# Left-factor sums in two rows, and another place for the turns of q and k

## The chip, the cores and the metric

The kernel runs on one core of a Trainium2 chip. A core has TensorE (PE in the profile, its weight loads PEld), VectorE (DVE), ScalarE (ACT), GpSimd (POOL) and SyncE (SP, which here only issues transfers). The engines run side by side, each through its own list of instructions in the order in which the program wrote them, and wait for each other by semaphores. TensorE writes into PSUM banks; in this kernel four are kept for scores, one for turns and values, three for products.

The metric is the device time of one execution in microseconds. The kernel before takes 1606.82 us, the median of three runs (1606.74 to 1608.88).

## The reference, cut to what matters

Attention with normed q and k, then a gated feed-forward layer, all in fp32:

```python
batch, n_heads, seq, head_dim = (8, 12, 448, 64)
n_tokens, d_model, d_ff = (3584, 768, 1536)

# attention, for each of 8 sequences and 12 heads
q_n, k_n = rmsnorm(q, g_q), rmsnorm(k, g_k)
scores = q_n @ k_n.T / sqrt(64)
attn = exp(scores - max(scores)); attn = attn / (sum(attn) + 1e-9)
attn_out = attn @ v                     # heads side by side give x: 3584 x 768

# feed-forward
xn = x / rms(x) * rms_g
g = xn @ w_gate
out = (g * sigmoid(g)) * (xn @ w_val) @ w_out
```

The weights come in as 64-bit floats and have to be turned into 32-bit ones on the chip.

## The kernel before

A block is one sequence; its twelve heads are worked in six pairs, so there are 48 pairs (`NPAIR` is 6). The attention of a block is laid between the steps of the feed-forward layer of the block before it. The first pairs, up to pair 6, have nothing to be laid between: they run alone. Matmuls of the feed-forward layer are done by a Strassen-like scheme in blocks 1 to 7: seven products in place of eight, at the price of sums and differences of the factors on VectorE. Those of the output product's left factors (h) are the `sums` of the change.

Every call of `pe(...)` is one step of TensorE. `after(n, fn)` puts work for other engines behind the n-th step from now. So these two decide the order in each engine's list.

```python
    def after(n, fn):
        due.append((now["t"] + n, fn))

    def pe(fn):
        now["t"] += 1
        fn()
        for item in [d for d in due if d[0] <= now["t"]]:
            due.remove(item)
            item[1]()
```

Turning q or k into the layout that the scores need, a score, and the end of a pair:

```python
    def turn(g, i):
        ...
        ps = (ps_m if todo else ps_f).tile([128, 512], F32, name="tr", tag="m" if todo else "f")
        for t in range(NK):
            nc.tensor.transpose(ps[:, t * 128:(t + 1) * 128], src[:, t * 2 * D:(t + 1) * 2 * D], ident)      # L527
        if i == 0:
            ...
            nc.scalar.activation(st["qT", g], ps[:, 0:S], ACT.Copy, scale=gqk[:, 0:1])                      # L532
            nc.vector.tensor_copy(st["kT", g][:, LAST], ps[:, S:])                                         # L533
        else:
            nc.vector.tensor_copy(st["kT", g][:, FULL], ps[:, FULL])                                       # L535

    def score(g, cs):                 # two heads for each c in cs; one PSUM bank of four for each
        ...
                nc.tensor.matmul(ps[:, 0:S], lhsT=kT[r, c * 128:(c + 1) * 128], rhs=qT[r, :], start=True, stop=True)   # L545
        for (c, j), ps in sc.items():
            ...
            nc.scalar.activation(e, ps[:, 0:S], ACT.Exp, scale=rs[:, n:n + 1])                             # L549
    ...
    def sums(g):                      # the denominators of pair g, then x
        ...                           # matmuls with ones into den (L610)
        if direct(g):
            nc.vector.reciprocal(rd, den[:, 0:S])                                                        # L614
        ...
        nc.vector.tensor_tensor(x, av[:, 0:S], rd, ALU.mult)                                             # L625
```

`rests(g)` (L575 to L590) does the scores of the last 64 rows of pair g and opens the sums `av` (L581) and `den` of pair g-1; `values(g)` (L597) adds the rest of `av`. `squares` takes squares of q and k on ScalarE (L484) and their sums on VectorE (L487); the power and the scaling of q follow on GpSimd (L506, L511). `rms_x` and `norm_x` norm x for the feed-forward layer (L645 to L663).

The conversion of the weights goes in steps too. Each call of `convert()` gives one piece to ScalarE (L740, L741), joins the one before it on VectorE with three instructions, and adds the one before that on GpSimd (L785):

```python
    def join(lo, hi, top):
        nc.vector.tensor_scalar(top.bitcast(F32), top.bitcast(F32), 122879.9921875, 2.0**-15, ALU.min, ALU.max)     # L746
        nc.vector.tensor_scalar(top, top, 3, 0x3FFFFFF8, ALU.logical_shift_left, ALU.bitwise_and)                 # L747
        nc.vector.scalar_tensor_tensor(top, hi, -(2**30), top, ALU.bitwise_and, ALU.bitwise_or)                   # L748

    def turns(n):
        for _ in range(n):
            convert()
```

One group of the feed-forward layer's first part in blocks 1 to 7. The seven products use three PSUM banks in turn, so that p5 takes the bank that p1 and p2 had, once `hand` has read it:

```python
    def quad(b, fp):
        ...
        def hand(gate, value, dst):
            ...
            nc.scalar.activation(th, gate, ACT.Tanh, scale=0.5)                                          # L921
            def rest():
                nc.vector.scalar_tensor_tensor(dst, th, 1.0, gate, ALU.add, ALU.mult)                    # L924
                nc.vector.scalar_tensor_tensor(dst, dst, 0.5, value, ALU.mult, ALU.mult)                 # L925
            after(1, rest)
        ...                           # p1, p6 (adds u2), p2 (hand of bank a), p7 (adds u3, L914), p5, p4, p3
        def sums():
            st["left_sums"] = now["t"]
            for pair in range(len(out_pairs(b))):
                ...
                nc.vector.tensor_tensor(of("S1"), of("A21"), of("A22"), ALU.add)                         # L983
                nc.vector.tensor_tensor(of("S2"), of("S1"), of("A11"), ALU.subtract)                     # L984
                nc.vector.tensor_tensor(of("S3"), of("A11"), of("A21"), ALU.subtract)                    # L985
                nc.vector.tensor_tensor(of("S4"), of("A12"), of("S2"), ALU.subtract)                     # L986

        def p3_last():
            p3()
            after(3, sums)

        return [p1, p6, p2, p7, p5, p4, p3_last]
```

Six groups (`fp`) follow each other in a block. A block has two pairs of rows to sum (`out_pairs`), block 4 one. In block 1 `derive` and `derive_o` (L858, L879) also make differences of the weights on VectorE after most steps, up to three a step; not in the step in which `sums` ran.

The loop over the pairs that run alone:

```python
        if g <= NPAIR:
            if g > 1:
                pe(lambda: turn(g + 1, 0))
                pe(lambda: turn(g + 1, 1))
            pe(lambda: score(g, (0,)))
            squares(g + 2, 0)
            squares(g + 2, 1)
            if g > 1:
                some_rests(g)
            pe(lambda: rests(g))
            pe(lambda: values(g - 1))
            ...
            turns(1 if g == 1 else 3 if g < NPAIR else 0)
            pe(lambda: sums(g - 1))
            pe(lambda: score(g, (1, 2)))
            turns(2 if g == 1 else 0)
            ...
            continue
```

Of the kernel before, what the change touches and what calls it, by code (L numbers as in the profile page):

```python
# [22 lines left out]
NPAIR = H // 2  # L23
# [312 lines left out]
def safe_scores(  # L336
# [42 lines left out]
# [11 lines that stand above are left out]
    NG = B * NPAIR  # L390
# [414 lines left out]
    def out_pairs(b):  # L805
        return (((0, 1),), ((-1, 0), (1, 2)), ((-1, 0), (1, 2)), ((0, 1), (2, 3)))[b % 4]

    def carries(b):
        return b % 4 < 2
# [97 lines left out]
    def quad(b, fp):  # L907

        bank, add = {}, {}
        shift = 64 * (b % 2)  # L910

        def plus(name, ps, other, dst=None):
            add[name] = tmp.tile([128, S], F32, name=name, tag=name, bufs=1) if dst is None else dst
            nc.vector.tensor_tensor(add[name], ps[:, 0:S], add[other], ALU.add)  # L914

        def hand(gate, value, dst):

            th = tmp.tile([128, S], F32, name="th", tag="th", bufs=2)
            n = gate.shape[-1] * (gate.shape[1] if len(gate.shape) == 3 else 1)
            th = th[:, 0:n] if len(gate.shape) == 2 else th.rearrange("p (r n) -> p r n", r=2)  # L920
# [8 lines that stand above are left out]
        def rows(fc):  # L929
            return st["h", b, fc][:, shift:shift + S]  # L930

        def p1():
            bank["a"] = product(b, fp, "A11", "B11")
            add["p1"] = tmp.tile([128, S], F32, name="p1", tag="p1", bufs=1)
            nc.scalar.copy(add["p1"], bank["a"][:, 0:S])

        def p6():
            bank["b"] = product(b, fp, "S2", "T2")
            plus("u2", bank["b"], "p1")

        def p2():
            product(b, fp, "A12", "B21", onto=bank["a"])
            for fc in (fp, fp + NFP):
                st["h", b, fc] = free_h.pop(0)
                if ("h", b - 1, fc) in st:

                    before = st.pop(("h", b - 1, fc))
                    if b % 2:
                        nc.gpsimd.tensor_copy(st["h", b, fc][:, 0:64], before[:, S - 64:S])
                    if carries(b - 1):  # L950
                        at = out_pairs(b - 1)[-1][1] + 1
                        nc.gpsimd.tensor_copy(carried[fc], before[:, at * 128:(at + 1) * 128])
                    free_h.append(before)
            hand(bank["a"][:, 0:HT], bank["a"][:, HT:S], rows(fp)[:, 0:HT])

        def p7():
            bank["c"] = product(b, fp, "S3", "T3")
            plus("u3", bank["c"], "u2")

        def p5():  # L960
            bank["e"] = product(b, fp, "S1", "T1")
            add["cc"] = tmp.tile([128, 2, S], F32, name="cc", tag="cc", bufs=1)
            plus("c22", bank["e"], "u3", dst=add["cc"][:, 1, :])

        def p4():
            bank["d"] = product(b, fp, "A22", "T4")
            plus("c21", bank["d"], "u3")
            after(1, lambda: hand(add["c21"][:, 0:HT], add["c21"][:, HT:S], rows(fp)[:, HT:S]))

        def p3():  # L970
            product(b, fp, "S4", "B22", onto=bank["e"])
            plus("c12", bank["e"], "u2", dst=add["cc"][:, 0, :])
            after(1, lambda: hand(add["cc"][:, :, 0:HT], add["cc"][:, :, HT:S], rows(fp + NFP).rearrange("p (r n) -> p r n", r=2)))

        def sums():

            st["left_sums"] = now["t"]
            for pair in range(len(out_pairs(b))):
                if fp == 0:
                    st["so", b, pair] = {name: room_so[3 * pair + i].rearrange("p (c n) -> p c n", c=NFP)  # L980
                                         for i, name in enumerate(("S1", "S2", "S4"))}
                of = lambda name: left_o(b, pair, name, fp)
# [4 lines that stand above are left out]

        def p3_last():
            p3()
            after(3, sums)  # L990

        return [p1, p6, p2, p7, p5, p4, p3_last]

# [248 lines left out]
    def some_rests(g):  # L1242
        b, hp = divmod(g, NPAIR)
        if g == 1:
            norm_rests(0, 4, NPAIR)
        elif hp in (3, 4):
            norm_rests(b + 1, 3 * (hp - 3), 3 * (hp - 2))
# [5 lines that stand above are left out]
# [22 lines left out]
    for g in range(NG + 1):  # L1275
        b, hp = divmod(g, NPAIR)
        if g:
            load_pair(g + 3)
        if hp == 2:
            for i in range(2):  # L1280
                load_rests(b + 1, i, nc.sync)
            load_v_rests(b + 1)
        if g == 0:
            pe(lambda: score(0, (0,)))
            pe(lambda: rests(0))
            pe(lambda: score(0, (1,)))
            pe(lambda: turn(1, 0))
            pe(lambda: score(0, (2,)))
            norm_rests(0, 2, 4)
            squares(2, 0)  # L1290
            squares(2, 1)
            pe(lambda: turn(1, 1))
            for _ in range(3):
                convert()
            load_pair(3)
            load_v(2)
            convert()
            load_rows()
            continue
        if g <= NPAIR:  # L1300
            if g > 1:
                pe(lambda: turn(g + 1, 0))
                pe(lambda: turn(g + 1, 1))
            pe(lambda: score(g, (0,)))
            squares(g + 2, 0)
            squares(g + 2, 1)
            if g > 1:
                some_rests(g)
            pe(lambda: rests(g))
            pe(lambda: values(g - 1))  # L1310
            if g == 1:
# [3 lines that stand above are left out]
            load_v(g + 2)  # L1315

            turns(1 if g == 1 else 3 if g < NPAIR else 0)
            pe(lambda: sums(g - 1))
            pe(lambda: score(g, (1, 2)))
            turns(2 if g == 1 else 0)  # L1320
            if g == 2:
                bound()
            continue

        if g == NPAIR + 1:
            pe(lambda: score(g, (0,)))
            pe(lambda: rests(g))
            pe(lambda: rms_x(0))
        else:
            pe(lambda: (rests(g), score(g, (0,)) if g < NG else None))  # L1330
        pe(lambda: values(g - 1))
        load_v(g + 2)
        if g == NPAIR + 1:
            pe(lambda: score(g, (1,)))
            pe(lambda: norm_x(0))
            pe(lambda: score(g, (2,)))
        pe(lambda: sums(g - 1))
        if g == NPAIR + 1:
            begin(0, 15)
            turns(3)  # L1340
        elif g < NG:
            pe(lambda: score(g, (1, 2)))
        st["block"] = now["t"]
        if hp:
            fill()
# [4 lines that stand above are left out]
            fill()  # L1350
            pe(lambda: turn(g + 1, 1))
            fill()
            continue
        fill(3)
        pe(lambda: turn(g + 1, 0))
        fill(1)
        pe(lambda: rms_x(b - 1))
# [3 lines that stand above are left out]
        fill(len(todo))  # L1361
        begin(b - 1, 16)
        pe(lambda: norm_x(b - 1))
        fill()
# [41 lines left out]
```

## Time and profile before

| what | before |
|---|---|
| time | 1606.82 us |
| span of the profiled run | 1605.0 us |
| granted clock of TensorE, mean | 0.997 |
| TensorE, matmuls | 1572.9 us, 98% |
| VectorE | 873.0 us, 54% |
| GpSimd | 659.5 us, 41% |
| ScalarE | 471.0 us, 29% |
| pairs that run alone | about 17 to 84 us |
| feed-forward of block 0, first product | first matmul (L1121) at 97.13 us |
| feed-forward of blocks 1 to 7, first product (L902) | 303.3 to 1543.5 us |

In the rows of a timeline the first number is the start in us from the start of the span, the second the duration; x12 means twelve records, of which an fp32 matmul leaves two. A bracket at the end gives the idle time of that engine just before, and what ended it. In the list of waits each row names who waited, for whom, and then us in total, how often, and the longest. In a row of windows the columns are the window, its length, the busy time of TensorE, its weight loads, VectorE, ScalarE and GpSimd (number of instructions in brackets), the granted clock, and the share and rate of the transfers.

### The profile page before, as it was taken

The numbers are of one execution on the slowest core, as the hardware profiler recorded it, in microseconds if no ns is written. First come the engines' busy times: TensorE is split into PE (matmuls) and PEld (weight loads), VectorE is DVE, ScalarE is ACT, GpSimd is POOL, SyncE is SP. The second block draws the span as 40 slices with busy tenths as digits, with TensorE's granted clock in tenths as the row PEclk, the third lists the DMA queues.
The fourth block names the chain that finished last, engine by engine and source line by source line (L and its number), as shares of the span: only waits on it lengthen the run. The fifth ranks groups of instructions, "written<-read, shape, count | busy, mean of one in ns | idle before, by whom it ended". The sixth has DMA issues, their size and how long they took to land.

```text
span 1605.0 us, 21557 instructions
## 1 busy us (share of the span) xinstructions
PE 1572.9 (98%) x7286; PEld 1113.5 (69%) x7286; DVE 873.0 (54%) x1556; ACT 471.0 (29%) x940; POOL 659.5 (41%) x712
## 2 busy tenths in 40 slices
PE   8989999999999999999999999999999999999998
PEld 4334445777756887568875688668885688859974
DVE  6878889578833566335563254535563345513531
ACT  6745555232222222222222222323322222101010
POOL 6857886645423443244433443344542342000000
PEclk9999999999999999999999999999999999999999
DMA  7647565866756554465544655484554544457652
GB/s 211 203 138 223 191 210 164 258 214 208 255 177 186 154 150 145 133 193 154 150 135 133 203 156 158 142 259 135 158 153 123 169 141 136 126 162 222 174 151 57
DMA packets 261996, 273.28 MB, mean 170 GB/s; under 512 B 78836, under 2 KB 258804, under 8 KB 261876
## 3 DMA queue, kind: packets, MB, share of 16 engines
q1 hardware_dynamic: 260948, 271.61, 56.3%
q8 instruction: 60, 0.98, 0.3%
q14 instruction: 60, 0.49, 0.1%
q10 hardware_dynamic: 800, 0.20, 0.1%
q0 software_dynamic: 128, 0.00, 0.0%
HBM read 232.40 MB, written 39.32 MB: 169 GB/s over the span
## 4 chain that ended last, share of the span: by engine, by line
PE 80%; DVE 5%; POOL 0%; DMA 0%; issue 0%; SPq 0%; ACT 0%; DVEq 0%; POOLq 0%
PE ff L902 40%; PE ff L1093 22%; PE sc L545 6%; PE av L597 5%; PE sc L575 2%; PE den L610 2%; PE tr L527 1%; PE ff L1003 1%; DVE top L747 1%; DVE top L748 1%; DVE top L746 0%; PE ff L1121 0%; DVE rd L618 0%; DVE h L925 0%; DVE h L924 0%
## 5 line engine op out<-in xcount | busy, mean ns | idle before, releaser
L902 PE MATMUL ff<-x,w 128*128 128x224 f32 x1878 | 381.5, 354 | 3.7 <-DVE h L925 2.6
L902 PEld LDWEIGHTS ff<-x,w 128*128 128x128 f32 x1878 | 351.3, 190 | 19.2 <-issue 11.7
L555 POOL TENSOR_TENSOR es<-e 128x448 f32<-128x448 f32 x82 | 92.1, 1144 | 493.7 <-ACT e L549 493.7
L902 PE MATMUL ff<-xs,w 128*128 128x224 f32 x1374 | 281.4, 353 | 2.9 <-DVE w L858 2.9
L902 PEld LDWEIGHTS ff<-xs,w 128*128 128x128 f32 x1374 | 258.1, 190 | 6.3 <-issue 6.0
L562 POOL TENSOR_TENSOR es<-es,e 64x448 f32<-64x448 f32 (+1 forms) x164 | 191.8, 1180 | 6.3
L618 DVE RECIPROCAL rd<-rd 128x448 f32<-128x448 f32 x41 | 121.0, 2952 | 112.2 <-ACT rd L617 112.2
L549 ACT ACTIVATE e<-sc,rs 128x448 f32<-128x448 f32 x288 | 161.9, 634 | 47.6 <-PE sc L545 46.2
L1093 PE MATMUL ff<-w,h 128*128 128x384 f32 x498 | 167.8, 487 | 0.6 <-ACT p L1072 0.6
L1093 PE MATMUL ff<-w,raw 128*128 128x384 f32 x468 | 159.5, 487 | 0.3 <-DVE y L1065 0.3
L1093 PEld LDWEIGHTS ff<-w,h 128*128 128x128 f32 x498 | 93.5, 190 | 64.5 <-issue 1.3
L545 PE MATMUL sc<-qT,kT 64*128 64x448 f32 x576 | 136.1, 572 | 1.9 <-ACT e L549 0.7
L1093 PEld LDWEIGHTS ff<-w,raw 128*128 128x128 f32 x468 | 87.6, 190 | 60.9 <-issue 2.6
L597 PE MATMUL av<-e,vt 128*64 128x448 f32 x576 | 118.8, 548 | 0.0
L506 POOL TENSOR_TENSOR rs<-ms,mhalf 128x12 f32<-128x12 f32 (+1 forms) x50 | 114.2, 2284 | 4.2
L1121 PE MATMUL ff<-x,w 128*128 128x448 f32 x288 | 113.6, 548 | 0.0
L545 PEld LDWEIGHTS sc<-qT,kT 64*128 64x128 f32 x576 | 52.8, 185 | 78.9 <-issue 70.0
L914 DVE TENSOR_TENSOR cc<-ff,u 128x448 f32<-128x448 f32 x84 | 52.4, 623 | 91.6 <-PE ff L902 91.4
L1121 PEld LDWEIGHTS ff<-x,w 128*128 128x128 f32 x288 | 54.1, 193 | 51.9 <-issue 50.1
L597 PEld LDWEIGHTS av<-e,vt 128*64 128x64 f32 x576 | 37.1, 136 | 75.6 <-issue 73.6
L785 POOL TENSOR_TENSOR w<-top,raw 128x384 int32<-128x384 int32 x63 | 67.0, 1078 | 39.2 <-DVE top L748 25.9
L631 POOL TENSOR_TENSOR ss<-ss,rd 128x448 f32<-128x448 f32 x40 | 46.2, 1155 | 80.1 <-ACT rd L630 79.3
(132 smaller groups left out, 1814.4 us busy)
## 6 DMA issues: line engine op xcount, KB each, us to landing
w<-kept SPq DMA_DIRECT2D x511, 192.0 KB, 2.7
w<-kept_o SPq DMA_DIRECT2D x296, 192.0 KB, 2.7
kept<-w SPq DMA_DIRECT2D x89, 192.0 KB, 3.9
qk<-in_q_dram SPq DMA_DIRECT2D x48, 192.0 KB, 2.9
qk<-in_k_dram SPq DMA_DIRECT2D x96, 96.0 KB, 3.2
vt<-in_v_dram SPq DMA_DIRECT2D x48, 192.0 KB, 2.5
raw<-in_moe_w_gate_dram SPq DMA_DIRECT2D x24, 384.0 KB, 4.7
raw<-in_moe_w_val_dram SPq DMA_DIRECT2D x24, 384.0 KB, 4.5
```

What stands on the lines that cost most here:

```text
L506: nc.gpsimd.tensor_tensor(st["rs", g][:, cols], ms, mhalf[:, cols], ALU.pow)
L545: nc.tensor.matmul(ps[:, 0:S], lhsT=kT[r, c * 128:(c + 1) * 128], rhs=qT[r, :], start=True, stop=True)
L549: nc.scalar.activation(e, ps[:, 0:S], ACT.Exp, scale=rs[:, n:n + 1])
L555: nc.gpsimd.tensor_tensor(es, st["e", g, 0, j], st["e", g, 1, j], ALU.add)
L562: nc.gpsimd.tensor_tensor(es[r], es[r], e[r], ALU.add)
L597: nc.tensor.matmul(av[own(j), 0:S], lhsT=vt[:, j, c], rhs=st["e", g, c, j], start=False, stop=(c == NK - 1), skip_group_check=True)
L618: nc.vector.reciprocal(rd, rd)
L785: nc.gpsimd.tensor_tensor(data(key).bitcast(I32), top, lo, ALU.add)
L902: nc.tensor.matmul(bank[:, w * HT:(w + 1) * HT], lhsT=wt[:, c * 128:(c + 1) * 128], rhs=x[:, c, :], start=onto is None and w == c == 0, st ...
L914: nc.vector.tensor_tensor(add[name], ps[:, 0:S], add[other], ALU.add)
L1093: nc.tensor.matmul(ps, lhsT=left_o(b, which, LEFT_O[name], c), rhs=data(("wo", b, name, c)), start=first and c == 0, stop=c == NFP - 1, sk ...
L1121: nc.tensor.matmul(bank[w][:, 0:S], lhsT=data(key)[:, c * 128:(c + 1) * 128], rhs=st["x", 0, half][:, c, :], start=half == c == 0, stop=ha ...
```

## The change

Two things are changed. The sums of the output product's left factors, up to eight instructions in one place, are given to VectorE in two rows of four: the first row at the third step after a group's last product, the second two steps later. It is meant to let what other engines wait for come between them. And the pairs that run alone go back to another order: the turns of q and k, which stood between the scores c=1,2 of one pair and c=0 of the next, come after the latter. With it, three conversions of weights stand behind the scores of pair 6 and no longer behind the start of block 0, and in pair 7 the residual scores come before score c=0.

```diff
-        def sums():
+        def sums(pair):
             st["left_sums"] = now["t"]
-            for pair in range(len(out_pairs(b))):
+            if pair < len(out_pairs(b)):
@@ def p3_last():
             p3()
-            after(3, sums)
+            after(3, lambda: sums(0))
+            after(5, lambda: sums(1))
@@ for g in range(NG + 1):
         if g <= NPAIR:
-            if g > 1:
-                pe(lambda: turn(g + 1, 0))
-                pe(lambda: turn(g + 1, 1))
             pe(lambda: score(g, (0,)))
             squares(g + 2, 0)
             squares(g + 2, 1)
             if g > 1:
+                pe(lambda: turn(g + 1, 0))
                 some_rests(g)
+                pe(lambda: turn(g + 1, 1))
             pe(lambda: rests(g))
@@
             pe(lambda: score(g, (1, 2)))
-            turns(2 if g == 1 else 0)
+            turns(2 if g == 1 else 3 if g == NPAIR else 0)
@@
+        pe(lambda: (rests(g), score(g, (0,)) if g < NG else None))
         if g == NPAIR + 1:
-            pe(lambda: score(g, (0,)))
-            pe(lambda: rests(g))
             pe(lambda: rms_x(0))
-        else:
-            pe(lambda: (rests(g), score(g, (0,)) if g < NG else None))
@@
         if g == NPAIR + 1:
             begin(0, 15)
-            turns(3)
```

## The prediction

> **What bounds the kernel now.** I read four views of the profile of before: the shares of busy time, the waits of TensorE, the timeline around the longest of these waits, and the timeline around one of the short ones. The busy shares and the chain come first:
>
> ```profile
> PE 1572.9 (98%) x7286; PEld 1113.5 (69%) x7286; DVE 873.0 (54%) x1556; ACT 471.0 (29%) x940; POOL 659.5 (41%) x712
> ...
> PE 80%; DVE 5%; POOL 0%; DMA 0%; issue 0%; SPq 0%; ACT 0%; DVEq 0%; POOLq 0%
> ```
>
> TensorE is busy in 1572.9 of 1605.0 us, and its matmuls fill 80% of the chain. The change leaves out no matmul, so all that it can give or take is in the 32 us in which TensorE stands still, and in what a stop costs afterwards. The view of waits names them (us in total, times, longest):
>
> ```profile
> PE tr L527 <- DVE kT L533: 7.7, 2, 6.9
> PE ff L902 <- DVE w L858: 2.9, 2, 1.5
> PE ff L902 <- DVE h L925: 2.6, 3, 1.0
> ...
> PE ff L902 <- DVE u L914: 1.1, 1, 1.1
> ```
>
> What is left out are waits of 1.9 us and less, most of them in the first 84 us. The reader is to see one wait of 6.9 us, three of up to 1.0 us on h (L925), and two that the change hardly touches (w, L858). Now the long wait, in the timeline (start, duration, instruction):
>
> ```profile
> 112.32 0.91 DVE L746 TENSOR_SCALAR xs<-xs 128x384 f32<-128x384 f32 x1
> 113.26 1.17 DVE L747 TENSOR_SCALAR xs<-xs 128x384 int32<-128x384 int32 x1
> 114.46 1.36 DVE L748 SCALAR_TENSOR_TENSOR xs<-raw,xs 128x384 int32<-128x384 int32 x1
> 115.75 0.21 DVE L533 COPY kT<-tr 128x64 f32<-128x64 f32 x1
> ...
> 116.01 0.90 PE L527 MATMUL tr<-ident,qk 128*128 128x128 f32 x3 [6.90 <-DVE kT L533]
> 116.71 8.74 PE L1121 MATMUL ff<-x,w 128*128 128x448 f32 x18
> ```
>
> The copy L533 frees the one PSUM bank in which q and k are turned. It takes 0.21 us, but stands behind six joins of converted weights (L746 to L748, one join is one of each) that VectorE began only at 100.96: 14.8 us of backlog. The windows show what follows the stop:
>
> ```profile
> 109.00:116.00 7.00, 0.11 (x1) 0.00 (x0) 6.86 (x9) 0.99 (x2) 5.98 (x6) 0.82 0.77 221
> 116.00:121.00 5.00, 4.99 (x10) 2.74 (x11) 4.86 (x11) 0.03 (x1) 4.68 (x5) 0.57 0.24 87
> ```
>
> Columns after the length: TensorE, its weight loads, VectorE (6.86 of 7), ScalarE, GpSimd, then the granted clock: 0.57 for the five us after the stop. The same three turns and 18 matmuls, 9.37 us here (116.01 to 125.38), took about 7.2 us at 224.6 to 231.8 at full clock. So the stop costs 6.9 + 2.1 = 9.0 us. Last, one of the short waits on h:
>
> ```profile
> 563.14 0.28 DVE L983 TENSOR_TENSOR raw<-h,h 128x128 f32<-128x128 f32 x1
> 563.46 0.29 DVE L984 TENSOR_TENSOR raw<-raw,h 128x128 f32<-128x128 f32 x1
> 563.66 0.28 DVE L985 TENSOR_TENSOR h<-h 128x128 f32<-128x128 f32 x1
> 563.87 0.28 DVE L986 TENSOR_TENSOR raw<-h,raw 128x128 f32<-128x128 f32 x1
> ...
> 564.62 0.39 DVE L925 SCALAR_TENSOR_TENSOR h<-h,ff 128x224 f32<-128x224 f32 x1
> ...
> 565.05 2.54 PE L902 MATMUL ff<-x,w 128*128 128x224 f32 x12 [0.85 <-DVE h L925]
> ```
>
> The four sums of the second row pair, 563.14 to 564.07, stand directly before h, which frees the PSUM bank that p5 waits for.
>
> **What the Trainium skill says.** "TensorE: Matmul & The Clock Gate", section "What's actually happening", says that an idle window of about 3.4 us puts the array back to half clock, and that a busy window of that length brings it back. The trace agrees: after 6.9 us of rest the clock is 0.57, and it is 1.00 from 121. The waits of up to 1.9 us are too short for it. "SBUF — State Buffer", section "SBUF: two separate sides", says that VectorE and GpSimd share a port pair which one of them holds for a whole instruction. The trace fits: L747 takes 0.36 us alone and 1.06 us while GpSimd adds (1.01 us). That is why six joins of 0.35 + 0.36 + 0.56 take 14 us here and not 8. The same TensorE page, section "Architectural detail: the array is 16× 32×32, not 1× 128×128", calls VectorE strictly first in, first out. So the place of an instruction in the list is what counts, and the change moves places.
>
> **The change part by part.** No instruction is added or removed on any engine. Three things move.
>
> *A, the order in pairs that run alone (17 to 84 us).* Before: scores c=1,2 of pair g; both turns of pair g+2; score c=0 of g+1. After: all six scores in a row, then the turns. From the starts of the scores (25.96, 36.17, 49.36, 60.95, 72.61, 83.27) the periods of before are 10.2, 13.2, 11.6, 11.7 and 10.7 us. The last has no wait, so 10.66 us is TensorE's own work, and the three middle ones hold 2.5, 0.9 and 1.0 us of waits. On ScalarE the exponentials of score c=0 now come before the copy of q and the square of x, which waits for VectorE's x. So the squares for the next norm no longer stand behind that wait, and VectorE's gap of 1.57 us ahead of L487 closes. In exchange kT (L533) waits for q's copy, which comes 0.8 us later. Worked through with the durations of before:
> - pair 2: the turn's wait of 1.9 us on the scaled q (L511, GpSimd) falls under the score, but av waits for x, and x comes after three joins and the reciprocal (2.95 us), which begin 0.3 us later: +0.3;
> - pairs 3 and 4: the joins start 0.7 us sooner, x is there when av asks for it, and a wait of about 0.1 us for a score's bank is new: -0.8 and -0.9;
> - pair 5: no wait to win, the same 0.1 us: +0.1.
>
> Sum -1.3 us.
>
> *B, three conversions move from after the start of block 0 (97 us) to pair 6 (about 87 us).* There VectorE stands idle for 2.92 and 3.73 us (ahead of L647 and L663). Three joins of 1.27 us fit between x at 87.1 and the norm at about 91.5; GpSimd's adds and power then end near 93, and TensorE asks for them only at 93.9. What it costs: the residual scores now stand ahead of score c=0 of pair 7, so av waits for x at 87.1 about 1.4 us instead of having other work; before lost 0.6 us at this place, and a row of small shifts leaves the first matmul of block 0 some 0.6 us later. What it gives: of six joins three are gone from the backlog. VectorE is free at about 101.7, does three joins (4 us alone, 6 with GpSimd in the way) and one h (0.6), and reaches L533 between 106.5 and 108.5. TensorE asks at 109.1 + 0.6 = 109.7. I leave 0.5 us of wait. The stop of 9.0 us goes, clock and all: +0.6 - 9.0 + 0.5 = -7.9 us.
>
> *C, the sums in two rows.* Blocks 1 to 7 have six groups each. Block 4 has one row pair, so 36 groups change. In each, four sums of 0.28 us (0.93 us in a row) go from before h of the gate to behind p5's own addition. h frees p5's bank 0.93 us sooner: the waits of 0.85, 0.72 and 1.04 us become about 0, 0 and 0.1: -2.5. The wait of 1.1 us on u in block 1 (406.91) has the same eight sums ahead of it: -1.0. The derived weights in block 1 lose one step, and their waits (2.9 us) I leave as they are. In the other 32 groups no one waits, and nothing is gained. Sum -3.5 us, of which I count 3.
>
> Together -1.3 - 7.9 - 3 = -12.2 us, which gives 1594.6; I write 1595.
>
> **The rivals.** *First: the stop at 116 returns elsewhere.* VectorE is busy 46.05 of 50 us between 100 and 150, and a TensorE that is 8 us ahead may catch up with it again, or ScalarE's copy of q may be late. For it: the whole stage is full. Against it: the joins that went earlier are work taken out of this stage, and kT L535 at 120.4 is needed only at 125.4. It would leave -5 instead of -12: 1602. *Second: the pairs alone get slower.* The order in before was perhaps chosen to give the exponentials (0.55 us each) time before the score's banks are used again. If each of five pairs waited 0.6 us for a bank, A would be +3, the total -8: 1599. Against it: the first exponential ends 1.6 us after the row of scores begins, when TensorE is just through with the four. *Third: the pair 7 seam.* If norm, power and scaling of x come late, block 0 starts up to 3 us later, and the total is -9: 1598. *Fourth: the second row of sums lands before an addition that TensorE then waits for.* For the addition after p4 there are 2.27 us of matmul between, against 1.15 us of sums; worth at most +1.
>
> **Range and chances.** All rivals at once would eat the gain and give about 1605; with the waits in A wholly gone (4.5 us) and nothing left of B and C it would be some 1588. So 1587 to 1605 for 8 in 10. For 2% either way 32 us are needed, as much as all of TensorE's standstill: 1% each.
>
> **What would show it.** A: scores of pairs 3 to 6 begin 10.7 us apart. B: no wait on kT L533 above 3 us, and a clock near 1.00 in the windows between 109 and 121; the first matmul of block 0 at 95 to 98 us. C: the waits on h and u vanish from TensorE's list. What would make it wrong: a new wait above 3 us in block 0, which brings the half clock with it, or a first matmul of block 0 after 99 us.

## The result, and the profile after

The changed kernel takes 1596.8 us (median of 4 runs, 1596.38 to 1597.13), against 1607.05 us before (4 runs, 1606.74 to 1608.88). The ratio is 0.9934, with a 95% interval of 0.9917 to 0.9951: 10 us faster, within 2%. I had said 1595, in a range of 1587 to 1605.

The profile of the changed kernel, first the shares of busy time, then the list of TensorE's waits (us in total, times, longest):

```profile
PE 1571.9 (99%) x7286; PEld 1113.4 (70%) x7286; DVE 872.6 (55%) x1556; ACT 470.3 (29%) x940; POOL 660.1 (41%) x712
```

```profile
PE ff L902 <- DVE cc L914: 1.5, 3, 0.5
...
PE av L581 <- issue: 1.2, 1, 1.2
PE rb L657 <- POOL rs L649: 1.0, 1, 1.0
PE tr L527 <- DVE kT L533: 0.9, 1, 0.9
```

The same 7286 matmuls take the same time within 1.0 us. The wait of 6.9 us on kT is gone (the one of 0.9 is another, late in block 0), and so are the waits on h and u. Three rows of these are new: av without a named releaser and rb on rs, both in pair 7, and three waits on cc, the additions for c22. A fourth new row, left out here, is one of 1.7 us of av in pair 2, where the turn had waited 1.9 us before. The place of the former stop, in the timeline of the changed kernel (behind the sums its line numbers are one higher than before, so L1122 is L1121 of before):

```profile
107.79 1.38 DVE L748 SCALAR_TENSOR_TENSOR xs<-raw,xs 128x384 int32<-128x384 int32 x1
109.10 0.21 DVE L533 COPY kT<-tr 128x64 f32<-128x64 f32 x1
...
109.87 0.49 PE L527 MATMUL tr<-ident,qk 128*128 128x128 f32 x3
110.20 6.93 PE L1122 MATMUL ff<-x,w 128*128 128x448 f32 x18
```

VectorE is done with kT 0.6 us before TensorE asks for the bank. The 18 matmuls take 6.93 us; before they took 8.74. The windows of the same stretch (length, TensorE, weight loads, VectorE, ScalarE, GpSimd, clock, transfers) have the clock at 1.00 and TensorE full:

```profile
109.00:116.00 7.00, 7.00 (x22) 3.67 (x21) 6.79 (x16) 1.45 (x3) 6.68 (x7) 1.00 0.21 73
116.00:121.00 5.00, 5.00 (x28) 1.64 (x28) 4.90 (x7) 3.00 (x7) 5.00 (x5) 1.00 0.57 172
```

To see where the time went I compared the start of the same TensorE instruction in both traces. There are 48 turns of the last rows (L531), one for each pair, and further marks where a stage begins:

| mark | before, us | after, us | after less before |
|---|---|---|---|
| scores c=1,2 of pair 1 | 25.96 | 26.39 | +0.43 |
| scores c=1,2 of pair 6 | 83.27 | 82.33 | -0.94 |
| first matmul of block 0 | 97.13 | 98.05 | +0.92 |
| residual scores of pair 8, after the former stop | 125.38 | 117.06 | -8.32 |
| turn in block 1, ahead of its last change | 394.25 | 386.00 | -8.25 |
| next turn | 425.62 | 417.00 | -8.62 |
| turn in block 2, after its wait on h | 593.17 | 584.41 | -8.76 |
| turn in block 3, after its wait on h | 790.99 | 782.09 | -8.90 |
| last turn, block 6 | 1323.15 | 1314.26 | -8.89 |
| last matmul, block 7 | 1597.20 | 1587.36 | -9.84 |
| end of the span | 1605.0 | 1595.3 | -9.7 |

So the pairs alone (A) gave 1.37 us, the seam at pair 7 took 1.86, the stop gave 9.24 (0.07 came back after it), and the sums (C) gave 1.6 up to the last matmul, of which 0.95 behind the last turn. The first 0.43 us are not from the change; they are taken up at the end. Without them the changed kernel is 10.3 us ahead at the last matmul.

### The profile page after: what moved, and what is told of

It reads as the page before. It is cut to its first block, busy times and chain, and to the rows that moved or that the text cites. A ratio compares the mean times of both kernels' runs of the same rounds, so it can differ in the third digit from the quotient of the medians.

```text
span 1595.3 us, 21559 instructions
## 1 busy us (share of the span) xinstructions
PE 1571.9 (99%) x7286; PEld 1113.4 (70%) x7286; DVE 872.6 (55%) x1556; ACT 470.3 (29%) x940; POOL 660.1 (41%) x712
## 4 chain that ended last, share of the span: by engine, by line
PE 78%; DVE 7%; DMA 1%; issue 1%; POOL 0%; SPq 0%; ACT 0%; DVEq 0%; POOLq 0%
PE ff L902 39%; PE ff L1094 22%; PE sc L545 6%; PE av L597 5%; PE sc L575 2%; PE den L610 2%; PE tr L527 1%; DVE top L747 1%; DVE top L748 1%; DVE top L746 1%; PE ff L1004 1%; DVE rd L618 1%; DVE h L925 0%; DVE h L924 0%; DMA w<-kept_o 0%
## 5 line engine op out<-in xcount | busy, mean ns | idle before, releaser
L1122 PE MATMUL ff<-x,w 128*128 128x448 f32 x288 | 111.8, 541 | 0.0
L1122 PEld LDWEIGHTS ff<-x,w 128*128 128x128 f32 x288 | 53.3, 190 | 50.8 <-issue 49.0
L631 POOL TENSOR_TENSOR ss<-ss,rd 128x448 f32<-128x448 f32 x40 | 46.6, 1165 | 82.7 <-ACT rd L630 82.7
L935 ACT COPY p<-ff 128x448 f32<-128x448 f32 x42 | 22.4, 533 | 192.6 <-PE ff L902 192.6
```

Of the source, the lines that this page charges most:

```text
L631: after(1 if soon else 4, lambda: (nc.gpsimd.tensor_tensor(ss, ss, rd, ALU.add), st.update({("summed", b): hp})))
L1122: nc.tensor.matmul(bank[w][:, 0:S], lhsT=data(key)[:, c * 128:(c + 1) * 128], rhs=st["x", 0, half][:, c, :], start=half == c == 0, stop=ha ...
```

## The experiments

Each kernel ran in several rounds beside the kernel before on the same chip. The ratios are to that kernel, with a 95% interval. None leaves out a part of the computation; one adds matmuls that nobody reads. After the first 12 us of the program the executions stand up to 3 us apart, so a step of 1 to 2 us is read from the marks inside the traces, counted from the first scores on, and not from medians alone.

My theory after the result: the stop on kT went because three joins went, and the clock with it; the seam costs more than I had said; the sums bring less because a new wait took the place of the old. The rivals were that the turns and exponentials of the pairs removed the stop, and that the sums had brought all of the listed 3.5 us, with the loss elsewhere.

**The sums alone.**

```diff
 # the kernel before
-            after(3, sums)
+            after(3, lambda: sums(0))
+            after(5, lambda: sums(1))
```

> The kernel before with the sums in two rows of four and nothing else of the change. Theory (the shifts of TensorE's marks between the two traces): the waits on h and u go, but waits of about 0.5 us on the addition for c22 (cc, L914) come in their place, so it gains 1.4 us and takes 1605.6. Rival (the list of waits alone): every wait on h and u that went is gained, 3.5 us, 1603.5; then the rest of the loss against my prediction lies in the seam at pair 7. The wait of 6.9 us on kT L533 stays in both.

Measured: 0.9992 (0.9984 to 1.0001), 1607.2 us against 1608.69. By the marks, blocks 1, 2, 3 and 6 gain 0.23, 0.16, 0.15 and about 1.0 us, 1.5 in all. The interval of the times includes no gain at all, so the marks alone show it. The waits on cc are in its list too (1.6 us, three times). The theory holds and the rival falls: nothing is hidden in the seam, since this kernel has the seam of before. The timeline of the changed kernel shows what takes the gain back in block 2:

```profile
555.08 0.39 DVE L925 SCALAR_TENSOR_TENSOR h<-h,ff 128x224 f32<-128x224 f32 x1
...
555.52 2.54 PE L902 MATMUL ff<-x,w 128*128 128x224 f32 x12
556.31 0.61 DVE L914 TENSOR_TENSOR u<-ff,u 128x448 f32<-128x448 f32 x1
556.84 0.28 DVE L983 TENSOR_TENSOR raw<-h,h 128x128 f32<-128x128 f32 x1
...
557.56 0.28 DVE L986 TENSOR_TENSOR raw<-h,raw 128x128 f32<-128x128 f32 x1
557.77 0.54 DVE L450 TENSOR_REDUCE msr<-sq 128x6 f32<-128x384 f32 x1
...
558.23 0.61 DVE L914 TENSOR_TENSOR cc<-ff,u 128x448 f32<-128x448 f32 x1
...
558.90 2.54 PE L902 MATMUL ff<-xs,w 128*128 128x224 f32 x12 [0.51 <-DVE cc L914]
```

The product at 555.52 no longer waits for h. But a turn of q lies between p2 and p7 in this group, so that the fifth step is p7 and not p5. The second row of sums (556.84 to 557.77) therefore stands, with a reduce of squares (L450), ahead of the addition for c22 (cc). p3 accumulates onto the bank that this addition has to read first, and waits 0.51 us. A correction belongs here: I wrote that p5 takes the bank of p1 and p2. By the order of the additions in both traces the product that waited for h is p4.

**All but the sums.**

```diff
 # the changed kernel
-            after(3, lambda: sums(0))
-            after(5, lambda: sums(1))
+            after(3, sums)
```

> The changed kernel with the sums back in one row of eight. Theory: everything up to the first matmuls after the former stop is as in the changed kernel, 8.3 us sooner than before, and the waits on h and u return: 1598.2. Rival: the two parts lean on each other (the sums' gain is there only when block 0 hands on an earlier VectorE), then it would take 1597 or below, or above 1600.

Measured: 1598.39 us, 0.9938 (0.9925 to 0.9952). The waits on h (2.6 us, three times) and u (1.1) are back. By the marks it is 8.7 us ahead of before at the last matmul. With the 1.5 us of the run before that makes 10.2 of the 10.3; the two parts do not lean on each other.

**The conversions alone.**

```diff
 # the kernel before
-            turns(2 if g == 1 else 0)
+            turns(2 if g == 1 else 3 if g == NPAIR else 0)
@@
             begin(0, 15)
-            turns(3)
```

> The kernel before with the three conversions given behind the scores of pair 6 in place of behind the start of block 0; the turns, the order in pair 7 and the sums stay as before. Theory: this alone takes the stop of 9 us away (wait on kT L533 below 1 us, clock 1.00 between 109 and 121), and costs about 1 to 1.9 us at the seam, because VectorE's joins now stand ahead of the norm of x and GpSimd's adds ahead of its power: 1599. Rival: the stop goes because the turns and exponentials of the pairs were moved, then it stays here and the time is 1607 or more.

Measured: 1599.89 us, 0.9952 (0.9938 to 0.9965), 8.8 us less than before by the medians. By the marks, which leave out the start, 7.4 of the 10.3 us come from moving three conversions. Its list of TensorE's waits:

```profile
PE ff L902 <- DVE h L925: 2.6, 3, 1.0
...
PE rb L657 <- POOL rs L649: 1.4, 1, 1.4
...
PE tr L527 <- DVE kT L533: 0.8, 1, 0.8
```

The stop is gone though turns and exponentials stand as before, so the rival falls. The wait of rb on rs is there: the seam's price comes with the conversions. By the marks (+0.38 ahead of the seam, +2.25 behind it) it is 1.87 us, the same as in the changed kernel.

**The turns alone.**

```diff
 # the kernel before, pairs 2 to 6
-            if g > 1:
-                pe(lambda: turn(g + 1, 0))
-                pe(lambda: turn(g + 1, 1))
             pe(lambda: score(g, (0,)))
@@
             if g > 1:
+                pe(lambda: turn(g + 1, 0))
                 some_rests(g)
+                pe(lambda: turn(g + 1, 1))
```

> The kernel before with only the turns of q and k after score c=0 in pairs 2 to 6; conversions, pair 7 and sums stay as before. Theory: 1.4 us between the scores of pair 1 and pair 6 are gained, the stop of 6.9 us and its slow clock stay: 1605.5. Rival: the order of before was there to give the exponentials time, and without it the pairs get slower: 1608 to 1610.

Measured: 1606.48 us, 0.9987 (0.9981 to 0.9994), 2.2 us less than before. From pair 1's scores (28.12) to pair 6's (84.04) it is 55.92 us, in place of 57.31: 1.39 us. Only pair 1 got slower, by 0.24 us; the others did not miss the time that the old order gave the exponentials. Another 0.6 us comes between there and pair 8, where this kernel has nothing changed. The stop is 6.90 us in this trace as in before, but the 18 matmuls behind it take less time here than in before (8.74), and in the trace of the sums alone, with the same stop, more:

```profile
117.47 8.18 PE L1121 MATMUL ff<-x,w 128*128 128x448 f32 x18
```

```profile
118.99 9.24 PE L1122 MATMUL ff<-x,w 128*128 128x448 f32 x18
```

Windows of 1 us show where the slow clock lies, first with the turns alone, then with the sums alone:

```profile
113.00:114.00 1.00, 0.00 (x0) 0.00 (x0) 0.99 (x2) 0.00 (x0) 1.00 (x2) 0.58 0.64 152
119.00:120.00 1.00, 1.00 (x3) 0.59 (x2) 0.93 (x3) 0.00 (x0) 0.92 (x2) 0.51 0.00 0
```

```profile
116.00:117.00 1.00, 0.00 (x0) 0.00 (x0) 0.97 (x2) 0.00 (x0) 1.00 (x2) 0.91 0.83 275
123.00:124.00 1.00, 1.00 (x3) 0.41 (x3) 0.97 (x3) 0.29 (x1) 0.92 (x3) 0.68 0.00 0
```

All windows between the two of a trace have 0.50, so a window of 0.58 has the half clock for 0.84 of its 1.00 us. The half clock begins 3.3 us after TensorE stopped here, 4.4 in before and 5.4 with the sums alone, and lasts 6.8 us in all three. The later it begins, the more of it falls on the matmuls behind the stop: 3.2, 4.3 and 5.4 us. Half of that is 1.6, 2.2 and 2.7 us, and by so much the turn and the matmuls are longer than in the changed kernel. So one and the same stop has three prices. The 0.6 us here are no gain of the change, and the trace of the sums alone loses 0.5 us in the same way.

**TensorE kept at work during the stop.**

```diff
 # the kernel before
             fill()
+            if g == NPAIR + 1:
+                keep_warm(28)          # 28 matmuls ident x ident, 128 columns, into a bank of the scores; nobody reads it
             pe(lambda: turn(g + 1, 1))
```

> The kernel before with 28 matmuls of 128 columns, whose result nobody reads, put on TensorE ahead of the turn that waits 6.9 us (some 6.7 us of work at 0.24 us each), so that TensorE does not stand still while VectorE works off its joins. Nothing is taken out. Theory: the stop costs its own length and 2.1 us of half clock afterwards; with the clock held at 1.00 the turns and 18 matmuls take 7.2 us in place of 9.4 and the kernel gains about 2 us. Rival: those matmuls were slow because VectorE or the weights' transfers held them, then their 9.4 us and the time stay, or the time grows by what the added matmuls overrun.

Measured: 1605.09 us against 1607.81, 0.9984 (0.9977 to 0.9991), with 28 matmuls more. Timeline and windows of this kernel:

```profile
111.04 6.41 PE L1245 MATMUL warm<-ident 128*128 128x128 f32 x56
118.15 0.55 PE L527 MATMUL tr<-ident,qk 128*128 128x128 f32 x3 [0.69 <-DVE kT L533]
118.53 6.93 PE L1121 MATMUL ff<-x,w 128*128 128x448 f32 x18
```

```profile
109.00:116.00 7.00, 7.00 (x51) 5.91 (x50) 6.86 (x8) 2.03 (x4) 6.05 (x6) 1.00 0.76 225
116.00:121.00 5.00, 4.30 (x24) 2.98 (x23) 4.90 (x9) 0.01 (x1) 4.68 (x6) 1.00 0.55 164
```

VectorE's backlog is as it was (6.86 of 7 us), and TensorE still gets its bank only when kT is copied, but the 18 matmuls that follow take 6.93 us and not 8.74. The marks move from +2.09 ahead of the stop to +0.02 behind it: 2.07 us, against the 2.1 that I had put down for the slow clock. That part of the stop's 9 us is shown to be the clock. The size, 2.1 us, is that of the one trace of before.

**One, two and three conversions.**

```diff
 # the kernel before, with n = 1 or 2 (3 is the run above)
-            turns(2 if g == 1 else 0)
+            turns(2 if g == 1 else n if g == NPAIR else 0)
@@
             begin(0, 15)
-            turns(3)
+            turns(3 - n)
```

> The kernel before with one of the three conversions moved ahead to pair 6. Theory: each joined piece is worth about 2.2 us of backlog where GpSimd is in the way, so the wait on kT falls to about 4.7 us, still long enough for the slow clock: gain 2.3 us. Rival: the stop is set by something other than the number of joins (the copy of q on ScalarE, a transfer), then it stays near 6.9 us.

> The kernel before with two of the three conversions moved ahead to pair 6. Theory: the wait on kT falls to about 2.5 us, which is too short for the slow clock, so the step from one to two conversions is worth more than the step from none to one: 2.2 + 2.1 us, a gain of 6.5 us in all. Rival: a loss of clock in proportion to the wait, then each step is worth the same 3 us.

Measured: one gives 1605.61 us, 0.9986 (0.9980 to 0.9993); two give 1602.78 us, 0.9971 (0.9961 to 0.9982). The turn after the stop, in the timeline with one conversion moved and then with two:

```profile
114.88 0.90 PE L527 MATMUL tr<-ident,qk 128*128 128x128 f32 x3 [4.96 <-DVE kT L533]
115.57 8.22 PE L1121 MATMUL ff<-x,w 128*128 128x448 f32 x18
```

```profile
112.67 0.55 PE L527 MATMUL tr<-ident,qk 128*128 128x128 f32 x3 [3.02 <-DVE kT L533]
113.06 8.62 PE L1121 MATMUL ff<-x,w 128*128 128x448 f32 x18
```

The wait falls from 6.90 to 4.96, 3.02 and nothing, so the number of joins sets it. From the end of x (L625) to the copy L533 VectorE takes 14.7, 12.8, 10.8 and 7.2 us with none to three moved: 1.9 us for each of the first two, 3.7 for the third. The marks behind the stop move by -2.1, -3.9 and -7.4 us (with the seam, which costs 0.35 us with one or two and 1.87 with three). The step I expected from one to two comes only from two to three. A loss of clock in proportion to the wait (the rival) is not what happens either: the slow clock takes 1.65 us of the turn and the 18 matmuls with one conversion moved, 1.75 with two and none with three. A wait of 3.02 us was still enough for the slow clock, as the windows of the kernel with two moved show:

```profile
110.00:112.00 2.00, 0.00 (x0) 0.00 (x0) 1.97 (x2) 0.00 (x0) 2.00 (x2) 1.00 0.80 230
112.00:114.00 2.00, 1.33 (x6) 0.80 (x7) 2.00 (x6) 0.00 (x0) 1.85 (x3) 0.91 0.74 254
114.00:116.00 2.00, 2.00 (x4) 0.97 (x3) 1.93 (x5) 0.00 (x0) 1.83 (x3) 0.50 0.04 14
116.00:118.00 2.00, 2.00 (x5) 0.95 (x4) 1.90 (x6) 0.80 (x2) 1.92 (x2) 0.74 0.00 0
```

TensorE is back at 112.67, and the clock drops after that, to 0.50.

**The second row of sums later.**

```diff
 # the changed kernel
-            after(5, lambda: sums(1))
+            after(7, lambda: sums(1))
```

> The changed kernel with the second row of sums at the seventh step in place of the fifth, so that it stands behind the addition for c22 (cc) in the crowded groups too. Theory: the waits of 0.5 us on cc L914 go, three of them, and the kernel gains 1 to 1.5 us on the changed one: a ratio to before of about 0.9927. Rival: the row meets another addition there (c21, c12) and TensorE waits for that instead: no gain, or a loss of up to 1 us.

Measured: 1596.43 us, 0.9929 (0.9915 to 0.9942). On another chip than the changed kernel's first runs this does not tell them apart, so both ran again, side by side:

> The changed kernel once more, beside the next three and the kernel before on one chip, so that steps of 1 to 2 us can be read: a ratio to before of 0.9934, as measured first, if the first microseconds of the program (which start up to 2 us apart in the traces) average out.

> The changed kernel with the second row of sums at the seventh step, once more. Theory: TensorE's marks in the two traces say that it gains 2.1 us on the changed kernel in blocks 1 to 3. Rival: the medians of the two on different chips differed by 0.4 us only; if the gain was the first microseconds' scatter, the two are equal here.

Measured: the changed kernel 1598.39 us, 0.9929 (0.9915 to 0.9942); with the later row 1594.99 us, 0.9916 (0.9902 to 0.9929). The intervals overlap, the marks are clear: against the trace of the changed kernel they agree within 0.04 us up to block 1, and then stand at -0.5, -1.3 and -2.07 after the crowded groups of blocks 1, 2 and 3. The timeline of the kernel with the later row, block 2 again:

```profile
555.80 0.61 DVE L914 TENSOR_TENSOR u<-ff,u 128x448 f32<-128x448 f32 x1
...
556.79 0.61 DVE L914 TENSOR_TENSOR cc<-ff,u 128x448 f32<-128x448 f32 x1
...
557.71 2.44 PE L902 MATMUL ff<-xs,w 128*128 128x224 f32 x12
558.13 0.28 DVE L983 TENSOR_TENSOR raw<-h,h 128x128 f32<-128x128 f32 x1
```

cc comes before the row, p3 starts at once, and no wait on cc is left in the list. So the waits on h and u were worth what I had said (0.92 us in block 2: 0.14 in the changed kernel, 0.78 more here); from block 1 to the last matmul this kernel gains 3.6 us on before, where the list of waits had given 3.5. The fifth step was the wrong place to collect it.

**The seam.**

```diff
 # the kernel with the later row
-            turns(2 if g == 1 else 3 if g == NPAIR else 0)
+            turns(2 if g == 1 or g == NPAIR else 0)
@@ pair 7
             pe(lambda: rms_x(0))
+            turns(1)
```

> As the one before, and of the three conversions behind pair 6 the third is given after the norm of x in pair 7. Theory: of the 1.9 us that the seam lost, 1.0 is TensorE's wait for GpSimd's power (rb on rs L649), which stands behind joins and adds; one join fewer ahead of it brings about 1 us. Rival: the third join then delays the scaling of x or the copy L533 by as much, and nothing is gained.

```diff
 # and with it, pair 7
-        pe(lambda: (rests(g), score(g, (0,)) if g < NG else None))
         if g == NPAIR + 1:
+            pe(lambda: score(g, (0,)))
+            pe(lambda: rests(g))
             pe(lambda: rms_x(0))
             turns(1)
+        else:
+            pe(lambda: (rests(g), score(g, (0,)) if g < NG else None))
```

> As the one before, and pair 7 has the order of before again: score c=0 ahead of the residual scores, so that TensorE has work while av waits for x. Theory: the other 0.9 to 1.2 us of the seam's loss goes too, 2 us below the changed kernel with the later row, 4 us below the changed kernel. Rival: TensorE only comes sooner to the next wait (rb on rs, or the turn on L533), and it is no faster than the one before.

Measured: 1593.73 us, 0.9907 (0.9892 to 0.9922), and 1593.34 us, 0.9901 (0.9886 to 0.9916). In before TensorE meets no wait at the norm of x for block 0, in the changed kernel it does (timelines, before first):

```profile
89.99 0.16 DVE L647 TENSOR_SCALAR ms<-msx 112x4 f32<-112x4 f32 x1 [2.92 <-PE msx L645]
...
93.24 0.60 PE L657 MATMUL rb<-ident,rs 112*128 112x112 f32 x4
```

```profile
92.39 0.56 DVE L748 SCALAR_TENSOR_TENSOR top<-raw,top 128x384 int32<-128x384 int32 x1
92.86 0.15 DVE L647 TENSOR_SCALAR ms<-msx 112x4 f32<-112x4 f32 x1
...
94.17 0.60 PE L657 MATMUL rb<-ident,rs 112*128 112x112 f32 x4 [1.03 <-POOL rs L649]
```

The third join holds ms until 92.86, and rb waits for the power behind it. With that join after ms, rb starts at 92.89 without a wait, and the marks gain 1.1 us: the theory. The old order in pair 7 takes away the wait of av too (1.2 us), but gains only about 0.4 us more by the marks (from +0.03 ahead of the seam to -1.47, against -0.17 to -1.27), and its median is 0.4 us lower, within the intervals. Most of it goes, as the rival says, into the next step: a wait of 0.5 us on the sum of squares (msx on ss L631) is new. The last version is the fastest of the study.

## Why the prediction was right

- *What bounds it.* Right: the matmuls took the same time in both kernels, and all of the difference is in TensorE's waits and in its clock.
- *A, -1.3 us.* Right in sum, -1.37, but by some luck, for its parts were not. Pair 1 lost 0.24 us, which I had not counted (a score waits for its bank); pairs 2 to 5 gave 0.05, 1.14, 0.22 and 0.20 where I had +0.3, -0.8, -0.9 and +0.1. Pair 4 still waits for x, and its residual scores can't run beside av. So the scores of pairs 3 to 6 begin 10.45, 11.44 and 10.46 us apart, and my sign of 10.7 came in two of three.
- *B, the stop, -8.5 us.* Right, and slightly too small: -9.24 from the first matmul to the residual scores of pair 8. Both terms are shown apart: 6.9 us of joins and 2.07 us of clock, the latter the size in one execution. The 0.5 us of wait that I left did not come, but the margin was thin: the three joins left took 6.7 us, where I had 4 to 6, and the copy began at 109.10, not at 106.5 to 108.5, 0.6 us before it was too late.
- *B, the seam, +0.6 us.* Mis-sized: +1.86, and the first matmul of block 0 came at 98.05, just outside my 95 to 98. The wait of av for x that I had counted came (1.20 us), and with it one that I had not. I had GpSimd's power end at 93 and TensorE ask at 93.9. The joins took 1.3, 3.6 and 1.9 us from 86.05 on, not 1.27 each, while GpSimd was adding at the same time; I had seen that effect in block 0 and not put it in here. rs came at 94.1, and rb waited 1.03 us. Stop and seam erred in opposite directions, so B in sum, -7.4 for -7.9, looks better than its terms.
- *C, -3 us.* The step that failed in size: -1.6. That the waits on h and u go was right. That the sums behind p5's addition harm nobody was not: in groups with a turn of q ahead of p7 (behind p2 in blocks 2 and 3, behind p1 in block 1) the fifth step lies ahead of that addition. The fourth group that had waited, in block 6, has such a turn too, but VectorE has less to do there (no reduces L487 and L450): cc ends at 1321.11, p3 starts at 1321.87 without a wait, and 0.95 us is gained. This was my fourth rival, which I had worked out for the addition after p4, not for that of p5, and called worth at most 1 us; by the run with the later row it cost 2.1, 0.5 to 0.8 in each of three blocks.
- *The rivals.* The stop did not return elsewhere: the marks hold at -8.3 through the whole of block 0. The pairs alone did not get slower in sum.
- *The range.* Its low end does not follow from its own terms: 1606.8 less 4.5, 9.0 and 3.5 us is 1590, not 1588.

The two terms that were too good (1.3 us at the seam, 1.4 in the sums) and the one that was too careful (0.7 us at the stop), with 0.43 us of start and about 0.2 behind the last matmul that the change does not explain, make up the difference between the 12.2 us worked out and the 9.7 us between the spans.

## What to carry to other kernels

On an engine that works strictly in order, a wait of 7 us can come from a copy of 0.2 us: look at what stands ahead of the releaser, not at the releaser, and move that work to where the engine stands idle, after a look at what comes next there (three joins in such a gap cost 1.03 us of wait). Place work by what it must stand behind, not by a count of steps: the same count fell behind an addition in one group and ahead of it in the next. And compare marks of the same instruction in two traces; with a start that scatters by 2 to 3 us it showed steps of 0.15 us that medians could not.

## What I had not expected of the hardware

A wait of 3.02 us on TensorE was enough for the half clock. "TensorE: Matmul & The Clock Gate" of the Trainium skill, section "What's actually happening", names an idle window of about 3.4 us; here a shorter rest was enough: the trace has the clock at 0.50 in 114 to 116 us after TensorE had rested from 109.65 to 112.67, and the matmuls 1.7 us late. The waits of up to 1.85 us between the start and the stop left it at 1.00.

The start of the program scatters as well. TensorE does some matmuls with an identity while q and k are loaded, and then waits for k. In the execution traced of before and in that of the kernel kept at work (which is the same program there):

```profile
6.61 0.52 PE L527 MATMUL tr<-ident,qk 128*128 128x128 f32 x3 [1.60 <-DMA qk<-in_k_dram]
6.97 1.28 PE L1240 MATMUL warm<-ident 128*128 128x128 f32 x10
```

```profile
7.17 0.52 PE L527 MATMUL tr<-ident,qk 128*128 128x128 f32 x3 [2.12 <-DMA qk<-in_k_dram]
7.52 2.11 PE L1240 MATMUL warm<-ident 128*128 128x128 f32 x10
```

In the second one TensorE rested 2.12 us, and behind that the view of windows has the clock at 0.50 (in before it is 1.00 there):

```profile
8.00:10.00 2.00, 2.00 (x11) 2.00 (x11) 1.74 (x6) 0.71 (x2) 1.83 (x3) 0.50 0.90 237
```

The ten records take 2.11 us in place of 1.28, and the first row of the last keys is turned at 11.72 in place of 9.53. But a late k is not what sets executions apart in general. In the traces of the sums alone, of the turns alone and of the changed kernel run again the wait for k is 1.59, 1.49 and 1.60 us, no longer than in before, and the ten records still take 2.34 us; in that of two conversions moved it is 1.80 us, and they take 1.28. What sets these 2 to 3 us stays open. Whether a longer run of those first matmuls would change them was not tried.
